# Loading a broadcast reciprocal over 128 partitions at once, and two weight loads moved in a queue

## The chip, the cores and the metric

The kernel runs on one core of a Trainium2 chip. The core has a matrix engine (TensorE, PE in the profile), a vector engine (VectorE, DVE), an activation engine (ScalarE, ACT), a general engine (GpSimd, POOL) and an engine that here only issues transfers (SyncE, SP). The engines run their own instruction streams in order and wait for one another by semaphores. Transfers between device memory and the on-chip memory of 128 partitions run on 16 DMA engines. The metric is the time of one execution on the device in microseconds (us), less is better.

## The reference

The program is one transformer block: layer norm with scale and shift from a conditioning vector, linear attention, then a second layer norm and a gated feed-forward network. Only the attention and the two gates matter here:

```python
mod = (_silu(c) @ w_mod).reshape(c.shape[0], 6, 1, -1)
sa, ca, ga, sb, cb, gb = (mod[:, i] for i in range(6))
h = _layernorm(x) * (1 + ca) + sa
# linear attention, 32 heads of 32
pq, pk = phi(q), phi(k)
kv = einsum('bhsd,bhse->bhde', pk, v);  z = einsum('bhsd->bhd', pk)
num = einsum('bhqd,bhde->bhqe', pq, kv)
den = einsum('bhqd,bhd->bhq', pq, z)[..., None] + 1e-06
x = x + ga * ((num / den) @ wo)
h = _layernorm(x) * (1 + cb) + sb
x = x + gb * ((_gelu(h @ w_gate) * (h @ w_up)) @ w_down)
```

There are 2,048 tokens of 1,024 features; the network's hidden width is 3,584. Inputs and outputs are bfloat16. In this listing the six slices and the transposes of the original are shortened.

## The kernel before, in words

Tokens are handled as 16 chunks of 128. Four chunks make a group (sg 0 to 3), and a group has two halves (h 0 and 1) of 256 tokens, `HW` in the code. The 1,024 features of q, k and the output are cut into 8 blocks g of 128, each with 4 heads (k 0 to 3, `HPG`) of 32.

The stages of the stretch in question come in this order. From about 128 us on, `m_tile` (matmuls at line 873) multiplies phi(k) transposed with the normed rows, in three column tiles for each g; 24 tiles run in all, first those of g 0 to 3, then the first tiles of g 4 to 7, then the others. ScalarE copies each result to `mb`; when the last tile of a g is copied, `m_t` has SP transpose it by DMA (line 678) into `mtb`, of which there are two buffers. `kv_prod` (matmuls at 891) multiplies that with the value weights, and VectorE masks it into `kvt` (895). `w2_pair` (1174) multiplies kvt with wo, which VectorE has first scaled by the first gate (`wofold`, 1180, from `gab`, a row that SP has loaded over all partitions at line 833). The list `HOOK` says after which tile each of these steps stands.

`den` (1201) computes the denominators of two groups on PE, 32 rows by 256 columns for each half of a group; VectorE adds 1e-6 and takes the reciprocal (1207), and SP stores the result to a scratch tensor in device memory, `scr_rd` (1209). `rb_load` (1221) then loads it back, so that each of the 32 partitions of a head holds that head's row: that is the broadcast over partitions. Its target `RB` is float32, has two buffers, one for even and one for odd groups, and holds two halves of 8 x 256 values for each partition. `pq_scale` (1234) multiplies phi(q) by it on VectorE, two g at a time, four instructions for a half. `wo_mm` (1242) multiplies the scaled phi(q) of a chunk with W2, in the order of g, and VectorE adds the result to x (1251, 1255). Chunks 0 and 1 belong to the first half of group 0, chunks 14 and 15 to the second half of group 3.

After this a chunk's second layer norm runs on ScalarE and GpSimd, and SP transposes it by DMA into `h2a` or `h2b` (678). VectorE and ScalarE scale and shift these, VectorE forms sums for the feed-forward products (`ss`, 1366, and `tp`, 1386, from the weights `wt` that SP loads at 1325), and PE starts the feed-forward (1411). In the first unit of the feed-forward, the list `ORD0` puts chunks 14 and 15 between the products, so their `wo_mm` (254.8 and 260.8 us) come last. The weights of the last matrix (`wd`, 1496) follow much later.

The second gate's row is made in two halves of 512 columns (j 0 and 1). For each, `gb_load` (761) loads two tiles `wmg` of 512 KiB from w_mod, and VectorE adds up eight weighted rows (`gb_acc`, 772 and 774). PE and SP turn the sums into a row that is stored to `scr_row` (827) and loaded over all partitions much later (`gbb`, 833). The first pair of loads is issued in tiles 1 and 2; the second load of each tile is issued as soon as its first content is used up.

All transfers of this stretch are issued by SP, in one queue and in the order of the program. SP has eight semaphores that its transfers use in turn; a transfer waits for the one eight places before it. The wait for a buffer stands in the same queue, so what is behind it waits too. The order of VectorE, ScalarE and GpSimd in this stretch isn't the program's: `reorder` simulates the stretch with a table of costs (`COST`) and due times and sorts the three engines' instructions by it. PE and SP keep the program's order.

Of the kernel before, what the change touches and what calls it, by code (L numbers as in the profile page):

```python
# [14 lines left out]
NSG = 4  # L15
CPG = NCH // NSG
SGW = P * CPG
NDC = D // P
NG = 8
HPG = 4  # L20
# [293 lines left out]
def bass_adaLN_cond__linear_attn_block__geglu_ffn__prompt_kernel(  # L314
# [12 lines left out]
    bf16, f32, f32r, i32 = dt.bfloat16, dt.float32, dt.float32r, dt.int32  # L327
    scr_row = nc.dram_tensor("scr_row", [3, 4, 512], f32).ap()
    scr_mod = nc.dram_tensor("scr_mod", [2, NDC, P], f32).ap()
    scr_rd = nc.dram_tensor("scr_rd", [NSG, 2, HPG, NG, SGW // 2 + 16], f32).ap()[:, :, :, :, 0:SGW // 2]  # L330
    with ExitStack() as es:
        es.enter_context(nc.allow_non_contiguous_dma(reason="1024 modulation values, laid out by partition"))
        arena = es.enter_context(nc.sbuf_tensor("arena", [P, ARENA_BYTES], dt.uint8, align_bytes=64))
# [4 lines left out]
        def at(name, shape, dty, off):  # L338
            return nc.alloc_sbuf_tensor_at(name, shape, dty, offset=ABASE + off, align_bytes=4)
# [33 lines left out]
        RB = [at(f"rb{i}", [P, 2, NG, SGW // 2], f32, OFF_RB[i]) for i in range(2)]  # L373
# [47 lines left out]
        def r_sm(name):  # L421
            return [(SMO[name], SMO[name] + SMSZ[name], name)]
# [30 lines left out]
        def r_wv(g):  # L453
            return [(OFF_WK + g * 2048, OFF_WK + (g + 1) * 2048, "wv")]
# [4 lines left out]
        def r_pq(sg, k0=0, k1=NG, s0=0, s1=SGW):  # L459
            return r_t8(PQO[sg], f"pq{sg}", k0, k1, s0, s1)  # L460
# [40 lines left out]
        def r_rb(i, h, g0=0, g1=NG):  # L501
            return [(OFF_RB[i] + (h * NG + g0) * 1024, OFF_RB[i] + (h * NG + g1) * 1024, f"rb{i}")]
# [17 lines left out]
        def pr(b):  # L520
            return [(b * 2048, (b + 1) * 2048)]
# [7 lines left out]
        sch = Sched()  # L529
        T, A, V, G, Q = PE_, ACT_, DVE_, POOL_, SP_  # L530
# [40 lines left out]
        def wm_dma(t, sl):  # L571
            return sch.dma(Q, lambda e: e.dma_start(WMST[sl][:], wm_v[:, :, t * 512:(t + 1) * 512]), wr=r_wm(sl), note=f"wm{t}")
# [22 lines left out]
        for q in range(1, 4):  # L595
            wmq_dma(q)
            for d0, d1 in ((2 * q, 2 * q + 1), (2 * q + 1, 2 * q + 2)):
# [8 lines left out]
               rd=r_sm("c8") + r_sm("ident"), pwr=pr(4))  # L606
# [4 lines left out]
               rd=r_sm("thc") + r_sm("chalf"), wr=r_sm("siluT"))  # L611
# [145 lines left out]
        def r_wmg(i, d0=0, d1=4):  # L757
            return [(HBO[3] + i * 4096 + d0 * 1024, HBO[3] + i * 4096 + d1 * 1024, f"wmg{i}")]

        def gb_load(j, q):  # L760
            sch.dma(Q, lambda e: e.dma_start(WMG[q][:], wm_v[:, 4 * q:4 * q + 4, (10 + j) * 512:(11 + j) * 512]), wr=r_wmg(q), note=f"wmg{j}.{q}")
# [6 lines left out]
        def gb_acc(j, dc):  # L768
            acc, rng = GA_[j]
            src, rs_ = WMG[dc // 4][:, dc % 4, :], r_wmg(dc // 4, dc % 4, dc % 4 + 1) + r_sm("silf")  # L770
            if dc == 0:
                sch.op(V, lambda e: e.tensor_scalar(acc[:, :], src, SILF[:, 0:1], None, op0=ALU.mult), rd=rs_, wr=rng, note=f"macc{6 + j}.0")
            else:
                sch.op(V, lambda e: e.scalar_tensor_tensor(acc[:, :], src, SILF[:, dc:dc + 1], acc[:, :], op0=ALU.mult, op1=ALU.add),
                       rd=rs_ + rng, wr=rng, note=f"macc{6 + j}.{dc}")
            if dc % 4 == 3 and j == 0:
                gb_load(1, dc // 4)

        def gb_hilo(j):
            acc, rng = GA_[j]  # L780
# [88 lines left out]
        def m_tile(g, k, bank, j):  # L869
            o_, n = MK[k]  # L870
            o = None
            for c_ in range(NCH):
                o = sch.op(T, lambda e, c_=c_: e.matmul(PS(bank, 0, n), PK[c_][:, g * P:(g + 1) * P], xrow(c_, o_, o_ + n),  # L873
                                                        start=(c_ == 0), stop=(c_ == NCH - 1)),
                           rd=r_pk(c_, g * P, (g + 1) * P) + r_xr(c_, o_, o_ + n), pwr=(pr(bank) if c_ == 0 else ()), note=f"m g{g} k{k} c{c_}")
            pset_writer(bank, o)
            w = n - (k == 0)
            sch.op(A, lambda e: e.activation(MB[g][:, o_:o_ + w], PS(bank, 0, w), ACTF.Copy), prd=pr(bank),
                   wr=[(OFF_MB[g] + o_ * 2, OFF_MB[g] + (o_ + w) * 2, f"mb{g}")], note=f"mcp{g}.{k}")
            if k == 0:  # L880
                sch.op(A, lambda e: e.activation(ZCOLS[:, g:g + 1], PS(bank, w, n), ACTF.Copy), prd=pr(bank), wr=r_smc("zcols", g, 4), note=f"zc{g}")

        def m_t(g):
            i = g % 2
            tdma(Q, MTB[i][:, :, :], MB[g][:, :], r_mb(g), r_mtb(i), f"mT{g}")
# [160 lines left out]
        def wofold(*kcs):  # L1046
            for kc in kcs:
                rg = r_wo(kc)
                sch.op(V, lambda e, kc=kc: e.tensor_tensor(WO[:, kc, :], WO[:, kc, :], GAB[:, :], ALU.mult),
                       rd=rg + R_GAB, wr=rg, note=f"wofold {kc}")  # L1050
# [66 lines left out]
        for c_ in range(10, NCH):  # L1117
            b = seq.index(("k", c_ // 2 * 2, 0)) - (9 if c_ % 2 else 12)
# [6 lines left out]
        for c_ in range(8, NCH, 2):  # L1125
            b = seq.index(("k", c_, 0)) - 3
# [10 lines left out]
        for g in range(NG):  # L1137
            task(nk + g // 2, lambda g=g: sch.dma(Q, lambda e: e.dma_start(WV[:, g, :, :], wqkv_v[:, :, 2 * D + g * P:2 * D + (g + 1) * P]),
                                                  wr=r_wv(g), note=f"wv{g}"))
# [54 lines left out]
        HW = SGW // 2  # L1194
# [16 lines left out]
            return store  # L1211

        o_rd = {}
        rb_ops = {}

        def rb_load(sg, hs=(0, 1)):
            i = sg % 2
            for h in hs:
                made = []
                for k in range(HPG):  # L1220
                    made.append(sch.dma(Q, lambda e, h=h, k=k: e.dma_start(  # L1221
                        RB[i][32 * k:32 * (k + 1), h, :, :],
                        scr_rd[sg, h, k:k + 1, :, :].to_broadcast([32, NG, HW])),
                        wr=r_rb(i, h) if k == 0 else (), deps=made[0].deps if k else [o_rd[sg // 2]], note=f"rb{sg}.{h}.{k}"))
                rb_ops[sg, h] = made

        GH = [((0, 2), (2, 4)), ((4, 6), (6, 8))]

        def pq_scale(sg, h, gs):
            i, t0 = sg % 2, h * HW  # L1230
            for g0, g1 in gs:
                ap = PQ[sg][:, g0:g1, t0:t0 + HW]
                rng = r_pq(sg, g0, g1, t0, t0 + HW)
                sch.op(V, lambda e, ap=ap, i=i, h=h, g0=g0, g1=g1: e.tensor_tensor(ap, ap, RB[i][:, h, g0:g1, :], ALU.mult),  # L1234
                       rd=rng + r_rb(i, h, g0, g1), wr=rng, deps=rb_ops[sg, h], note=f"pqs{sg}.{h}.{g0}")

        def wo_mm(c_, b0, gs):
            sg, ci = divmod(c_, CPG)
# [47 lines left out]
        for n, (g, k) in enumerate(tiles):  # L1286
            m_tile(g, k, n % 4, n % 2)
            if k == 2:
                m_t(g)
            for _ in range(3):  # L1290
                mod_step()
            if 2 <= n <= 9:
                wofold(n - 2)
            while pend and n > 1:
                wm_dma(*pend.pop(0))
            if n in (1, 2):
                gb_load(0, n - 1)
            for f in HOOK.get(n, "").split():
                hook_run(f)
        for i in range(4):  # L1300
            pq_scale(0, i // 2, GH[i % 2])
# [6 lines left out]
        kv_prod(7, 5)  # L1308
        w2_pair(6)
        rb_load(1)  # L1310
        x_dma(NXR, 10)
        wo_mm(2, 4, E6[:4])
# [356 lines left out]
```

## Time and profile before

| | |
|---|---|
| time, median of 3 runs | 806.04 us (804.77 to 806.11) |
| the profiled execution | 806.37 us, its span 804.5 us |
| granted TensorE clock | 1.00 in the whole span |
| bytes moved by DMA | 97.73 MB, mean 121 GB/s |
| rb loads | 32 of 256 KB, median 5.4 us from issue to landing |
| wmg loads | 4 of 512 KB, median 6.0 us |
| transposes into mtb | 8, median 5.1 us, longest 10.3 us |

The span is the time from the first to the last instruction of the program; the time on the clock is 1.87 us longer in the profiled execution. The profile gives each engine's busy time. PE's share is near the whole, so the rest of the profile is read for the short stretches in which PE isn't busy, and for what ended them.

The stretch around the change is seen best in the queue of SP. The columns are start, duration, engine and line, operation, target and source, and number of instructions; some rows are left out.

```profile
136.42 0.35 SPq L833 DMA_DIRECT2D gab<-scr_row  x1
136.83 0.42 SPq L761 DMA_DIRECT2D wmg<-in_w_mod_dram  x1
137.35 1.28 SPq L678 DMA_TRANSPOSE mtb<-mb  x1
138.73 0.52 SPq L572 DMA_DIRECT2D wmst<-in_w_mod_dram  x1
139.30 3.31 SPq L761 DMA_DIRECT2D wmg<-in_w_mod_dram  x1
142.71 0.45 SPq L572 DMA_DIRECT2D wmst<-in_w_mod_dram  x1
143.26 9.25 SPq L678 DMA_TRANSPOSE mtb<-mb  x2
163.44 0.37 SPq L761 DMA_DIRECT2D wmg<-in_w_mod_dram  x1
163.92 1.24 SPq L678 DMA_TRANSPOSE mtb<-mb  x1
...
178.75 2.01 SPq L1221 DMA_DIRECT2D rb<-scr_rd  x4
181.91 1.23 SPq L678 DMA_TRANSPOSE mtb<-mb  x1
183.19 2.08 SPq L1221 DMA_DIRECT2D rb<-scr_rd  x4
...
196.06 3.93 SPq L1221 DMA_DIRECT2D rb<-scr_rd  x8
...
213.13 2.01 SPq L1221 DMA_DIRECT2D rb<-scr_rd  x4
```

Here the wmg loads stand between the gab load and the second transpose, and the third wmg load ahead of the transpose of g 3. Each half of the broadcast is four issues. Three further groups of four rb loads, at 223.1, 226.6 and 241.0 us, stand between the transposes of h2 and the loads of x and wt.

### The profile page before, as it was taken

Reading aid. Unit: us, or ns where it says so; the run is one execution under the profiler, and the core shown is the slowest. Engines: PE = TensorE matmul, PEld = TensorE weight load, DVE = VectorE, ACT = ScalarE, POOL = GpSimd, SP = SyncE. Lnnn points to the kernel's source line nnn. Section 1 sums busy time; section 2 is a strip of 40 time slices with the busy share of each in tenths; the row PEclk is TensorE's granted clock in tenths of the full one; section 3 lists DMA queues with packets and bytes.
Section 4 is the critical chain, followed back from the end, with each engine's and each line's share of the span. In section 5 each row is a group of like instructions: output and inputs, shape, how many; then the busy total and the mean of one; then the engine's idle time right before and its main releaser. Section 6 shows DMA issues by size and latency. Waiting matters only on the chain.

```text
span 804.5 us, 10875 instructions
## 1 busy us (share of the span) xinstructions
PE 792.9 (99%) x4029; PEld 465.3 (58%) x4029; DVE 568.1 (71%) x1008; ACT 303.1 (38%) x511; POOL 39.4 (5%) x102
## 2 busy tenths in 40 slices
PE   7999999999999999999999999999999999999998
PEld 4444445666444677767775444467776777744445
DVE  6699898984699978788786375577887878601422
ACT  2497743232655444344443410033544435300000
POOL 2121200000320000000000000000000000000000
PEclk9999999999999999999999999999999999999999
DMA  9789859749898135323237324022231323430100
GB/s 282 242 176 231 176 116 230 186 98 184 186 265 225 53 112 150 98 61 104 58 101 235 53 74 110 20 86 76 82 105 53 106 72 86 136 126 7 53 20 27
DMA packets 168508, 97.73 MB, mean 121 GB/s; under 512 B 68476, under 2 KB 156804, under 8 KB 168456
## 3 DMA queue, kind: packets, MB, share of 16 engines
q1 hardware_dynamic: 168440, 97.04, 47.0%
q8 instruction: 32, 0.52, 0.3%
q14 instruction: 20, 0.16, 0.1%
q10 hardware_dynamic: 16, 0.00, 0.0%
HBM read 78.92 MB, written 4.47 MB: 104 GB/s over the span
## 4 chain that ended last, share of the span: by engine, by line
PE 84%; DMA 6%; SPq 4%; DVE 3%; issue 1%; ACT 1%; POOL 0%; DVEq 0%; POOLq 0%; ACTq 0%
PE ps_all L1411 43%; PE ps_all L1496 24%; PE ps_all L909 7%; PE ps_all L858 6%; PE ps_all L873 3%; DMA rb<-scr_rd 3%; DMA mtb<-mb 1%; SPq L575 1%; DVE pq L1234 1%; DMA wmq<-in_w_mod_dram 1%; SPq L580 1%; DVE ss L1366 1%; SPq L1221 1%; DMA scr_row<-mrowa 1%; SPq L678 1%
## 5 line engine op out<-in xcount | busy, mean ns | idle before, releaser
L1411 PE MATMUL ps_all<-ss,tp 128*128 128x512 f32 x896 | 224.7, 402 | 1.2 <-DVE ss L1366 1.2
L1496 PE MATMUL ps_all<-wd,yT 128*128 128x512 bf16 (+3 forms) x952 | 193.9, 366 | 0.0
L1411 PEld LDWEIGHTS ps_all<-ss,tp 128*128 128x128 f32 x896 | 168.2, 188 | 42.4 <-DVE ss L1366 2.6
L1496 PEld LDWEIGHTS ps_all<-wd,yT 128*128 128x128 bf16 x952 | 90.0, 98 | 103.8 <-ACT ge L1427 0.5
L1427 ACT ACTIVATE ge<-ps_all 128x512 f32<-128x512 f32 x112 | 64.2, 597 | 144.7 <-DVE ps_all L1422 79.7
L1411 PE MATMUL ps_all<-h2a,wt 128*128 128x512 bf16 x448 | 106.2, 380 | 0.4 <-DVE xall L1255 0.4
L1386 DVE TENSOR_TENSOR tp<-wt 128x512 fp32r<-128x512 bf16 x112 | 74.3, 688 | 39.6 <-PE ps_all L1411 20.8
L1431 DVE TENSOR_TENSOR yT<-ge,ps_all 128x512 bf16<-128x512 f32 x112 | 74.7, 685 | 34.4 <-PE ps_all L1411 31.0
L1422 DVE TENSOR_TENSOR ps_all<-ps_all,es 128x512 f32<-128x512 f32 x112 | 75.3, 696 | 16.1 <-PE ps_all L1411 16.1
L1488 DVE TENSOR_TENSOR ps_all<-ps_all,gbb 128x512 f32<-128x512 f32 (+3 forms) x34 | 22.7, 668 | 79.0 <-PE ps_all L1496 79.0
L1386 DVE TENSOR_TENSOR tp<-wt,tp 128x512 fp32r<-128x512 bf16 x112 | 72.0, 684 | 0.0
L1411 PEld LDWEIGHTS ps_all<-h2a,wt 128*128 128x128 bf16 x448 | 39.4, 98 | 55.0 <-issue 14.8
L1242 PE MATMUL ps_all<-w,pq 128*128 128x512 bf16 x256 | 56.5, 379 | 1.6 <-DVE pq L1234 1.6
L858 PE MATMUL ps_all<-wk,h1T 128*128 128x512 bf16 x248 | 56.8, 379 | 0.3 <-DVE h1T L699 0.2
L909 PE MATMUL ps_all<-h1T,wq 128*128 128x512 bf16 x256 | 56.7, 379 | 0.0
L1411 PE MATMUL ps_all<-ar,tp 128*128 128x512 f32 x224 | 55.3, 389 | 0.0
L1416 ACT ACTIVATE ps_all<-ps_all 128x512 f32<-128x512 f32 x56 | 32.6, 582 | 53.2 <-PE ps_all L1411 51.4
L847 ACT ACTIVATE eb<-ps_all 128x512 f32<-128x512 f32 x64 | 36.4, 594 | 37.7 <-PE ps_all L858 15.6
L1411 PEld LDWEIGHTS ps_all<-ar,tp 128*128 128x128 f32 x224 | 42.0, 188 | 8.7
L1242 PEld LDWEIGHTS ps_all<-w,pq 128*128 128x128 bf16 x256 | 24.7, 98 | 32.0 <-DVE pq L1234 2.3
L909 PEld LDWEIGHTS ps_all<-h1T,wq 128*128 128x128 bf16 x256 | 24.9, 98 | 30.0
L1419 ACT ACTIVATE es<-ps_all 128x512 f32<-128x512 f32 x56 | 33.5, 601 | 18.6 <-PE ps_all L1411 18.6
(118 smaller groups left out, 638.0 us busy)
## 6 DMA issues: line engine op xcount, KB each, us to landing
wt<-in_B_w_gate_dram SPq DMA_DIRECT2D x28, 512.0 KB, 4.2
wt<-in_B_w_up_dram SPq DMA_DIRECT2D x28, 512.0 KB, 4.9
wd<-in_B_w_down_dram SPq DMA_DIRECT2D x12, 1024.0 KB, 7.3
rb<-scr_rd SPq DMA_DIRECT2D x32, 256.0 KB, 5.4
wmst<-in_w_mod_dram SPq DMA_DIRECT2D x6, 1024.0 KB, 5.6
wmq<-in_w_mod_dram SPq DMA_DIRECT2D x8, 512.0 KB, 6.1
out_dram<-xall SPq DMA_DIRECT2D x31, 128.0 KB, 1.7
xall<-in_A_x_dram SPq DMA_DIRECT2D x5, 512.0 KB, 4.1
```

The lines of the kernel that those rows point to most:

```text
L847: sch.op(A, lambda e: e.activation(EB[i][:, :], PS(bank), ACTF.Exp), prd=pr(bank), wr=rng, note=f"{note}.exp")
L858: o = sch.op(T, lambda e, dc=dc: e.matmul(PS(bank), H1[sg][:, ci, dc, :], W_[:, dc, jg * 512:(jg + 1) * 512], start=(dc == 0), stop=(dc == ...
L909: o = sch.op(T, lambda e, dc=dc: e.matmul(PS(b), WQ[:, dc, qc * P:(qc + 1) * P], H1[sg][:, :, dc, :], start=(dc == 0), stop=(dc == NDC - 1 ...
L1242: last[half] = sch.op(T, lambda e, g=g, half=half: e.matmul(PS(b0 + half), PQ[sg][:, g, ci * P:(ci + 1) * P], W2[:, g, half * 512:(half + ...
L1386: sch.op(V, lambda e, t=t: e.tensor_tensor(TP[k][:, t, :, :], in0[:, t, :, :], in1[:, t, :, :], ALU.subtract), rd=r0[t:t + 1] + (r1[t:t + ...
L1411: o = sch.op(T, lambda e, l_=l_, r_=r_, dc=dc: e.matmul(PS(b), l_, r_, start=fresh and dc == 0, stop=dc == ND2 - 1, skip_group_check=True) ...
L1416: sch.op(A, lambda e: e.activation(PS(BB + t), PS(BA + t), ACTF.Copy), prd=pr(BA + t), pwr=pr(BB + t), note="pcp")
L1419: sch.op(A, lambda e: e.activation(ES[t][:, :], PS(BE + t), ACTF.Copy), prd=pr(BE + t), wr=r_2k(OFF_ES[t], f"es{t}"), note="escp")
L1422: sch.op(V, lambda e: e.tensor_tensor(PS(dst + t), PS(BB + t), ES[t][:, :], ALU.add), prd=pr(BB + t), rd=r_2k(OFF_ES[t], f"es{t}"), pwr=pr ...
L1427: sch.op(A, lambda e: e.activation(GE[i][:, :], PS(b), ACTF.Gelu_apprx_tanh), prd=pr(b), wr=r_2k(OFF_GE[i], f"ge{i}"), note="gelu")
L1431: sch.op(V, lambda e: e.tensor_tensor(YT[:, yrow(fc), h * SGW:(h + 1) * SGW], GE[i][:, :], PS(b + 1), ALU.mult), rd=r_2k(OFF_GE[i], f"ge{i ...
L1496: o = sch.op(T, lambda e, fc=fc: e.matmul(PS(b, 0, n), YT[:, yrow(fc), ci * P:(ci + 1) * P], WDT[fc // 4][:, fc % 4, c0:c1], start=first a ...
```

## The change

The change has three parts. First, `rb_load` loads a half with two transfers in place of four. Each covers all 128 partitions and four of the eight blocks g, and its source pattern has three levels: the four heads k, 32 repeats of each, and 1,024 values in one piece. `pq_scale` now waits only for the transfer that holds its own blocks. Second, the scratch tensor loses the 16 values of padding that followed each row of 256. Third, the wmg loads move in SP's queue: the first pair is issued in tiles 6 and 7, behind the transpose of g 1, and the second pair in tile 11, behind that of g 3.

```diff
-    scr_rd = nc.dram_tensor("scr_rd", [NSG, 2, HPG, NG, SGW // 2 + 16], f32).ap()[:, :, :, :, 0:SGW // 2]
+    scr_rd = nc.dram_tensor("scr_rd", [NSG, 2, HPG, NG, SGW // 2], f32).ap()
...
-            if dc % 4 == 3 and j == 0:
-                gb_load(1, dc // 4)
...
         def rb_load(sg, hs=(0, 1)):
             i = sg % 2
             for h in hs:
-                made = []
-                for k in range(HPG):
-                    made.append(sch.dma(Q, lambda e, h=h, k=k: e.dma_start(
-                        RB[i][32 * k:32 * (k + 1), h, :, :],
-                        scr_rd[sg, h, k:k + 1, :, :].to_broadcast([32, NG, HW])),
-                        wr=r_rb(i, h) if k == 0 else (), deps=made[0].deps if k else [o_rd[sg // 2]], note=f"rb{sg}.{h}.{k}"))
-                rb_ops[sg, h] = made
+                for q in range(2):
+                    src = scr_rd[sg, h, :, 4 * q:4 * q + 4, :].rearrange("k (o g) t -> k o (g t)", o=1).to_broadcast([HPG, 32, 4 * HW])
+                    sch.dma(Q, lambda e, h=h, q=q, src=src: e.dma_start(RB[i][:, h, 4 * q:4 * q + 4, :].rearrange("p a b -> p (a b)"), src),
+                            wr=r_rb(i, h, 4 * q, 4 * q + 4), deps=[o_rd[sg // 2]], note=f"rb{sg}.{h}.{q}")
...
-                       rd=rng + r_rb(i, h, g0, g1), wr=rng, deps=rb_ops[sg, h], note=f"pqs{sg}.{h}.{g0}")
+                       rd=rng + r_rb(i, h, g0, g1), wr=rng, note=f"pqs{sg}.{h}.{g0}")
...
-            if n in (1, 2):
-                gb_load(0, n - 1)
+            if n in (6, 7):
+                gb_load(0, n - 6)
+            if n == 11:
+                gb_load(1, 0)
+                gb_load(1, 1)
```

Since the planner simulates the new transfers, it also puts some of VectorE's instructions in another order: the product of the mask with z, two of the folds of wo, the reciprocal of the second pair of groups and the masks of kvt 5 to 7 stand elsewhere. The masks of kvt 5 to 7 now follow all eight `pq_scale` instructions of group 0. On ScalarE the copies into `mb` and the roundings of the sums change places a few times. The order of PE is the same.

More of the change, by code (lines that the diff above doesn't have):

```diff
@@ L1213, in bass_adaLN_cond__linear_attn_block__geglu_ffn__prompt_kernel @@
         o_rd = {}
-        rb_ops = {}
         def rb_load(sg, hs=(0, 1)):
```

## The prediction

> **What bounds the kernel now.** I read the busy times first, then the chain of waits, then the timelines of TensorE (PE), VectorE (DVE) and the SyncE queue (SP) between 125 and 262 us, where the change lies, and last the DMA view over short windows.
>
> ```profile
> span 804.5 us, 10875 instructions
> PE 792.9 (99%) x4029; PEld 465.3 (58%) x4029; DVE 568.1 (71%) x1008; ACT 303.1 (38%) x511; POOL 39.4 (5%) x102
> ```
>
> PE is busy 99% of the span, so an edit can win only PE's gaps, but it can lose as much as it holds PE up. The PE timeline names the gaps in this stage; the bracket at the end of a row gives the idle time before it and who ended it.
>
> ```profile
> 153.58 0.62 PE L891 MATMUL ps_all<-mtb,wv 128*128 128x128 bf16 x8 [1.11 <-DMA mtb<-mb]
> 231.87 13.99 PE L1242 MATMUL ps_all<-w,pq 128*128 128x512 bf16 x64 [1.59 <-DVE pq L1234]
> 254.84 3.63 PE L1242 MATMUL ps_all<-w,pq 128*128 128x512 bf16 x16
> ```
>
> Further gaps of 0.44, 0.72, 0.17 and 0.30 us lie at 246.3, 250.6, 252.9 and 258.8: 4.33 us in all. That is the most the change can win. The rb loads are ahead of two DVE stalls and of the 1.59 us gap:
>
> ```profile
> 220.73 2.50 DVE L1234 TENSOR_TENSOR pq<-pq,rb 128x512 bf16<-128x512 bf16 x4 [3.00 <-DMA rb<-scr_rd]
> 231.12 2.50 DVE L1234 TENSOR_TENSOR pq<-pq,rb 128x512 bf16<-128x512 bf16 x4 [1.14 <-DMA rb<-scr_rd]
> 252.76 2.49 DVE L1234 TENSOR_TENSOR pq<-pq,rb 128x512 bf16<-128x512 bf16 x4
> ```
>
> The DMA engines are the second limit: from 213 to 258 us their busy share is 111.9%. So what a load costs the queue matters. Four windows price it: 131 to 136.4 us (the end of the two wo loads, and the four-row store of mrowa), 137 to 141.2 (the gab load, then wmg), 198.4 to 206 (rb loads alone), 248.4 to 250.7 (the gbb load between wt loads).
>
> ```profile
> DMA packets 806, 1.57 MB, mean 291 GB/s; under 512 B 36, under 2 KB 40, under 8 KB 806
> DMA packets 510, 0.89 MB, mean 212 GB/s; under 512 B 25, under 2 KB 382, under 8 KB 510
> DMA packets 1755, 1.69 MB, mean 222 GB/s; under 512 B 105, under 2 KB 1755, under 8 KB 1755
> DMA packets 656, 0.88 MB, mean 381 GB/s; under 512 B 32, under 2 KB 474, under 8 KB 655
> ```
>
> Present price: 1 MiB of rb (one half of one group of four chunks) at 222 GB/s is 4.7 us; eight such halves are 8 MiB. The first row holds something more. Its 36 smallest packets are no data; two loads over 128 rows and one store over 4 rows ended there, and 36 = 16 + 16 + 4. I read them as one completion word per DMA engine that took part: 16 engines for a transfer whose outermost count is 128, 4 for one whose outermost count is 4.
>
> **The change, part by part.**
>
> *The rb loads.* Each half becomes 2 DMAs of 512 KiB instead of 4 of 256 KiB. That takes two SP issues of about 0.45 us from each half (a group of four takes 2.01 us), lets the first two scalings of a half start when half its bytes are there, and makes the packets 4 KiB instead of 1 KiB. But the source pattern changes too. Before, its outermost count was 32 (one row of 1/den repeated 32 times). Now it is 4 (k), then 32 repeats, then 1,024 floats; the destination still counts 128. If the smaller outermost count decides, as in the four-row store, only 4 of the 16 engines carry 1/den.
>
> Price on 4 engines: gbb is the row most like the new load (512 KiB, 4 KiB packets, one row repeated over partitions). Its window ran at 381 GB/s, 23.8 per engine; times 4 that is 95.3 GB/s, so 1 MiB takes 11.0 us. The bad end is the gab window, the same kind of load at 212 / 16 = 13.25 per engine: 19.8 us. On 16 engines 1 MiB takes 2.75 us (381) to 4.9 (212). I take 4 engines at 11.0 us.
>
> [...]
>
> Now the queue. Every later DMA puts a sixteenth of itself on each of the four slow engines, behind the rb packets there, so those four set the pace. From the first rb half (issued 178.75; gab's bytes began to move about 1.2 us after issue, so 180.0) to the end of the last, they carry 8 x 11.0 = 88.0 us of rb. Queued between are 11 transposes of 256 KiB (three mtb, eight h2), x loads of 1,792 KiB, wt loads of 1,024 KiB and the 128 KiB store: 5.9 MB at 264 GB/s, the mean of 131 to 147 us, 22.3 us. End: 180.0 + 88.0 + 22.3 = 290.3. For this the four must never run dry. The closest call is h2a's first transpose, which needs chunk 0. DVE now puts kvt5 to kvt7 behind all eight scalings of group 0, so W2 of g 5 (PE at 193.3) waits until the second half lands at 180 + 22.0 + 1.4 = 203.4, near 204.5: 11 us late. The transpose (issued 211.8) then comes at about 223, while the four engines have work until about 228. It holds.
>
> What is late next: the scalings of chunks 14 and 15 need the last half. PE reaches that point at 254.84 now and finishes chunk 14 at 258.47. Then: last bytes at 290.3, one scaling 0.63, the remaining four g of chunk 14 at 8 x 0.216 (a chunk's 16 matmuls take 3.45 us) = 1.73, end 292.7: 34.2 us late. DVE's sums of h2 stand ahead of these scalings and themselves wait for h2 transposes queued behind rb; they take 0 to 2 us more, I take 0.8. After that nothing is left to hide the loss, because PE has no gap from 264 us on. Sum: 804.5 + 35.0 = 839.5 us of span. The span stands 1.5 us below the median shown (806.04), so the forecast is 841 us.
>
> *w_mod loads of the second gate.* Two wmg loads (1 MiB) leave the queue ahead of the transpose mtb of g 1, which takes 10.28 us from issue to landing and causes the 1.11 us gap. At 264 GB/s they are worth 4.0 us of its wait, so the gap goes: -1.11 us on PE. Their own landing is hidden: the first use is at 158.9 on DVE, and from 155 to 165 us the DMA share is 0.04, so all that is queued here ends before. Without this cover DVE, which has no idle from 141.4 to 172, would wait up to the 4.0 us. The second pair now issues after the transpose of g 3, whose issue no longer waits at 163.44 for DVE's sums; kv3 on PE was not waiting for it, so it wins nothing. This gain starts the rb queue at most 1.1 us earlier; I leave it inside the range.
>
> *Planner and padding.* DVE moves the z product and two folds of wo, and puts the second reciprocal behind two scalings; its store leaves SP at 195.4, 10 us after the reciprocal, so that is hidden in front of rb1. Dropping 64 bytes of padding leaves the stores' bytes the same: 0.
>
> **The rivals.**
>
> *A, all 16 engines carry the new loads (it ends faster).* For it: the destination counts 128. Against: the four-row store. A half then takes 2.75 us, the waits for rb vanish, and up to 4.33 us of gaps go: 800.2 to 804 of span, 801.7 to 805 on the clock. It decides as long as 1 MiB stays under the 4.7 us of today. 11%.
>
> *B, four engines for each load, but different ones in turn.* Consecutive halves then overlap and 1 MiB costs about 2.75 to 5.5 us: 804.5 to 807.5. Nothing in the profile speaks for it; the four-row stores show the number of engines, not which. 4%.
>
> *C, four engines at the lower rate of gab.* 8 x (19.8 - 11.0) = 70 us on top: 911. For it: rb itself runs at 13.9 per engine. Against: four engines read four different rows here, and gbb, with all on one row, ran at full rate. 5%.
>
> *D, 16 engines, but kvt5 behind the scalings costs PE 1 to 3 us:* 806 to 809. 2%. The forecast itself has 78%.
>
> **How the numbers follow.** The likeliest case alone lies between 825 and 866: rb rows overlap by 12.9% in busy share (-10 us), the other loads may pass at some 346 GB/s, as in the last slices of 131 to 147 us (-5); up to 14.2 us per MiB, midway in rate between gab and gbb, adds 25. The range goes to 880 for part of C and leaves out A, B and D and the tails, about 2 in 10: 825 to 880. About 0.2% (1.6 us) is what a measurement of this kernel can tell from no change. Faster: A, 11%. Same: most of B, 4%. Slower: the forecast, C, D and the rest, 85%.
>
> **What would show it.** Right: rb landings of 10 us and more; DMA busy share near 0.3 while rb moves, at about 95 GB/s; PE gaps before L1242 that sum to some 35 us between 190 and 295, ended by the scalings or by transposes; no gap at 153.6 before L891. Wrong: rb windows near 381 GB/s and a DVE without waits at the scalings (then A), or a share near 0.3 with PE not held up (then the queue does not run in order).

## The result, and the profile after

| | before | after |
|---|---|---|
| time, median of the runs beside each other | 806.08 us (804.77 to 806.18, 4 runs) | 852.95 us (852.07 to 854.16, 4 runs) |
| ratio, 95% interval | | 1.0591 (1.0578 to 1.0604) |
| span of the profiled execution | 804.5 us | 850.3 us |
| granted TensorE clock, mean | 1.00 | 0.974 |

The kernel became 5.9% slower; the span grew by 45.8 us. The busy times on the page of the kernel after:

```profile
PE 804.7 (95%) x3962; PEld 469.4 (55%) x4029; DVE 569.0 (67%) x1008; ACT 302.9 (36%) x511; POOL 38.1 (4%) x102
```

PE's share fell from 99% to 95%, and its busy time rose although the work is the same. Both mean lost time: the first is idle time, the second is slower matmuls. VectorE's timeline shows what it waited for. Columns: start, duration, engine and line, operation, tiles, count, and in brackets the idle time before and who ended it.

```profile
242.27 1.29 DVE L1228 TENSOR_TENSOR pq<-pq,rb 128x512 bf16<-128x512 bf16 x2 [6.03 <-DMA rb<-scr_rd]
247.27 1.29 DVE L1228 TENSOR_TENSOR pq<-pq,rb 128x512 bf16<-128x512 bf16 x2 [3.70 <-DMA rb<-scr_rd]
...
298.16 1.29 DVE L1228 TENSOR_TENSOR pq<-pq,rb 128x512 bf16<-128x512 bf16 x2 [3.71 <-DMA rb<-scr_rd]
```

The two loads of a half land 5.00 us apart, so 512 KiB take 5.0 us and a half of 1 MiB takes 10.0 us, against 4.7 us before. Fourteen such waits add up to 49.6 us. The last two scalings, for which chunks 14 and 15 wait, start at 298.16 us. The DMA view of the stretch from 196 to 205 us, in which most of one half of 1/den moves beside little else, gives the rate:

```profile
DMA packets 856, 0.94 MB, mean 105 GB/s; under 512 B 665, under 2 KB 669, under 8 KB 855
q1 hardware_dynamic: 855, 0.93, 30.8%
```

The 16 engines are busy for 30.8% of that stretch, though a load is under way for nearly all of it. Rate and share are those of 4 or 5 engines out of 16. The completion words that the prediction counted decide between the two. The end of one load in the kernel after (198.4 to 199.2 us) and of one in the kernel before (199.3 to 199.9 us):

```profile
DMA packets 24, 0.08 MB, mean 102 GB/s; under 512 B 4, under 2 KB 4, under 8 KB 24
DMA packets 131, 0.12 MB, mean 196 GB/s; under 512 B 16, under 2 KB 131, under 8 KB 131
```

The packets under 512 B, of 4 bytes each, are the completion words: 4 now, 16 before. PE's timeline shows what this did to the matmuls:

```profile
206.58 0.63 PE L1172 MATMUL ps_all<-wo,kvt 128*128 128x512 bf16 x1 [9.17 <-DVE kvt L893]
...
259.50 3.60 PE L1236 MATMUL ps_all<-w,pq 128*128 128x512 bf16 x8 [4.34 <-DVE pq L1228]
277.26 5.35 PE L1236 MATMUL ps_all<-w,pq 128*128 128x512 bf16 x24 [3.11 <-DVE pq L1228]
298.91 3.08 PE L1236 MATMUL ps_all<-w,pq 128*128 128x512 bf16 x8 [3.11 <-DVE pq L1228]
```

Twelve gaps between 192 and 304 us, four of them shown, sum to 34.3 us, against 4.33 us of gaps before: 30.0 us more. The rows also show slower matmuls: 8 of them take 3.60 or 3.08 us, where a chunk's 16 took 3.45 us before. The view by windows shows why; its columns are the stretch, the busy time of each engine with its count, the granted clock, the DMA share and the rate:

```profile
195.00:205.00 10.00, 2.42 (x10) 1.06 (x8) 1.67 (x3) 0.46 (x1) 0.00 (x0) 0.67 0.31 102
215.00:225.00 10.00, 9.95 (x48) 4.42 (x47) 5.85 (x11) 3.94 (x5) 1.70 (x5) 1.00 0.52 146
300.00:306.00 6.00, 5.02 (x12) 2.91 (x11) 6.00 (x8) 0.60 (x1) 0.00 (x0) 0.50 0.80 226
```

Where PE waited, the mean granted clock of the window fell to 0.67; where it was fed (215 to 225 us), it was 1.00. It stayed at 0.50 for a while after the last wait. The busy time of PE is best compared with a kernel in whose trace as many matmul records, 67 of 4,029, are missing: the last experiment below has 3,962 as well, and 788.2 us. The slow clock thus made PE's work some 16.5 us longer. Gaps and slower work together are 30.0 + 16.5 = 46.5 us, within 0.7 us of the growth of the span.

### The profile page after: what moved, and what is told of

It is laid out like the page before. It is cut to its first block, busy times and chain, and to the rows that moved or that the text cites. A ratio compares the mean times of both kernels' runs of the same rounds, so it can differ in the third digit from the quotient of the medians.

```text
span 850.3 us, 10784 instructions
## 1 busy us (share of the span) xinstructions
PE 804.7 (95%) x3962; PEld 469.4 (55%) x4029; DVE 569.0 (67%) x1008; ACT 302.9 (36%) x511; POOL 38.1 (4%) x102
## 3 DMA queue, kind: packets, MB, share of 16 engines
q1 hardware_dynamic: 161848, 97.03, 49.6%
## 4 chain that ended last, share of the span: by engine, by line
PE 82%; SPq 7%; DMA 7%; DVE 1%; issue 1%; ACT 1%; POOL 0%; ACTq 0%; POOLq 0%; DVEq 0%
PE ps_all L1408 41%; PE ps_all L1493 23%; PE ps_all L907 7%; PE ps_all L871 6%; SPq L678 5%; PE ps_all L856 4%; DMA rb<-scr_rd 4%; DMA h2a<-xl 2%; PE ps_all L1236 2%; SPq L575 1%; DMA wmq<-in_w_mod_dram 1%; SPq L580 1%; SPq L1218 0%; ACT xl L649 0%; SPq L569 0%
## 5 line engine op out<-in xcount | busy, mean ns | idle before, releaser
L1408 PE MATMUL ps_all<-h2a,wt 128*128 128x512 bf16 x420 | 101.6, 384 | 4.2 <-DVE xall L1249 2.2
L1236 PE MATMUL ps_all<-w,pq 128*128 128x512 bf16 x251 | 67.1, 427 | 18.8 <-DVE pq L1228 18.4
L1236 PEld LDWEIGHTS ps_all<-w,pq 128*128 128x128 bf16 x256 | 26.5, 107 | 58.5 <-DVE pq L1228 23.6
L1228 DVE TENSOR_TENSOR pq<-pq,rb 128x512 bf16<-128x512 bf16 x32 | 20.6, 688 | 49.6 <-DMA rb<-scr_rd 49.6
```

What stands on the lines that cost most here:

```text
L1236: last[half] = sch.op(T, lambda e, g=g, half=half: e.matmul(PS(b0 + half), PQ[sg][:, g, ci * P:(ci + 1) * P], W2[:, g, half * 512:(half + ...
L1408: o = sch.op(T, lambda e, l_=l_, r_=r_, dc=dc: e.matmul(PS(b), l_, r_, start=fresh and dc == 0, stop=dc == ND2 - 1, skip_group_check=True) ...
```

## The experiments

All times stand beside runs of the kernel before on the same chip (medians of 805.2 to 805.6 us).

**1. Only the w_mod loads moved.**

```diff
 (before)
-            if dc % 4 == 3 and j == 0:
-                gb_load(1, dc // 4)
...
-            if n in (1, 2):
-                gb_load(0, n - 1)
+            if n in (6, 7):
+                gb_load(0, n - 6)
+            if n == 11:
+                gb_load(1, 0)
+                gb_load(1, 1)
```

> The rb loads, the padding and the waits of the kernel before; only the w_mod loads of the second gate are moved behind the transposes. Theory (the rb loads alone cost the 47 us): 1.1 us faster than before at most, 804.5 to 806.5 us, no gap of PE before L891 at 153.6. Rival (the moved w_mod loads, or the order of VectorE that the planner makes of them, carry part of the loss): more than 3 us slower than before.

Measured: 804.72 us (804.00 to 805.88, 11 runs), ratio 0.9994 (0.9985 to 1.0003). No difference that can be told: the moves carry none of the loss, and no gain that shows.

**2. Only the loads of 1/den changed** (the kernel after, with `gb_load` where it was before).

```diff
 (after)
-            if n in (6, 7):
-                gb_load(0, n - 6)
-            if n == 11:
-                gb_load(1, 0)
-                gb_load(1, 1)
+            if n in (1, 2):
+                gb_load(0, n - 1)
...
+            if dc % 4 == 3 and j == 0:
+                gb_load(1, dc // 4)
```

> The new rb loads and no padding, with the w_mod loads where they were before. Theory: the whole loss, 851 to 856 us, each 512 KiB of rb in 5.0 us. Rival (as for the run with the w_mod loads alone): clearly under 850 us.

Measured: 853.46 us (851.64 to 854.53, 4 runs), ratio 1.0596 (1.0581 to 1.0611). The new loads carry the whole loss.

**3. Four copies of 1/den, so that the source's outermost count is 16.** The loads keep their number, their 128 partitions and their 4 KiB packets; SP issues four stores where it issued one.

```diff
 (after)
-    scr_rd = nc.dram_tensor("scr_rd", [NSG, 2, HPG, NG, SGW // 2], f32).ap()
+    scr_rd = nc.dram_tensor("scr_rd", [NSG, 2, HPG, 4, NG, SGW // 2], f32).ap()
...
-    src = scr_rd[sg, h, :, 4 * q:4 * q + 4, :].rearrange("k (o g) t -> k o (g t)", o=1).to_broadcast([HPG, 32, 4 * HW])
+    src = scr_rd[sg, h, :, :, 4 * q:4 * q + 4, :].rearrange("k r (o g) t -> (k r) o (g t)", o=1).to_broadcast([16, 8, 4 * HW])
```

> As the changed kernel, but 1/den is stored four times (four stores for one), so that the loads' source pattern is 16 rows, 8 repeats, 1,024 values: 128 partitions and 4 KiB packets as before, outermost count 16 instead of 4. Theory (the outermost count of the source sets the number of DMA engines, 4 in the changed kernel): 16 engines, 1 MiB in 2.7 to 4.9 us, VectorE's waits for rb nearly gone, PE's clock full, 800 to 806 us. Rival 1 (4 KiB packets of a repeated row, or the lost padding, are slow whatever the count): 845 us or more. Rival 2 (the destination's count of 128 differs from the source's, and that alone makes the transfer slow): 845 us or more too.

Measured: 809.11 us (806.99 to 809.56, 5 runs), ratio 1.0038 (1.0024 to 1.0052), above the theory's 800 to 806. VectorE's timeline and the DMA view of 187.5 to 192 us of this kernel:

```profile
190.77 1.29 DVE L1228 TENSOR_TENSOR pq<-pq,rb 128x512 bf16<-128x512 bf16 x2 [1.43 <-DMA rb<-scr_rd]
193.06 1.29 DVE L1228 TENSOR_TENSOR pq<-pq,rb 128x512 bf16<-128x512 bf16 x2 [0.99 <-DMA rb<-scr_rd]
```

```profile
DMA packets 313, 1.05 MB, mean 234 GB/s; under 512 B 57, under 2 KB 57, under 8 KB 313
q1 hardware_dynamic: 313, 1.05, 104.6%
```

A load now lands 2.29 us after the one before it, not 5.00, it ends in 16 completion words (189.59 to 189.70 us), all engines are busy, and almost the whole loss is gone. So it was the source's outermost count of 4 that made the loads slow, not their 128 partitions nor their size. But the rate is only about that of the old loads over 32 partitions (222 GB/s), and the kernel is still 0.4% slower than before.

**4. Two copies, outermost count 8.**

```diff
 (after, as in 3 with 2 in place of 4)
+    src = scr_rd[...].rearrange("k r (o g) t -> (k r) o (g t)", o=1).to_broadcast([8, 16, 4 * HW])
```

> The same with two copies: 8 rows, 16 repeats, 1,024 values. Theory: 8 engines, so 512 KiB in about 2.5 us and 1 MiB in 5.0 us, close to the 4.7 us of the kernel before: 803 to 812 us. Rivals 1 and 2: 845 us or more. If the number of engines isn't set by the count, no value between the run with four copies and the changed kernel is explained.

Measured: 834.61 us (833.81 to 835.29, 4 runs), ratio 1.0364 (1.0350 to 1.0378), far above what was expected. VectorE's timeline and the DMA view of 191.5 to 199.5 us of this kernel:

```profile
195.42 1.29 DVE L1228 TENSOR_TENSOR pq<-pq,rb 128x512 bf16<-128x512 bf16 x2 [4.32 <-DMA rb<-scr_rd]
199.82 1.29 DVE L1228 TENSOR_TENSOR pq<-pq,rb 128x512 bf16<-128x512 bf16 x2 [3.11 <-DMA rb<-scr_rd]
```

```profile
DMA packets 494, 0.89 MB, mean 111 GB/s; under 512 B 294, under 2 KB 294, under 8 KB 494
q1 hardware_dynamic: 494, 0.89, 52.7%
```

The share of 52.7% is that of 8 engines, as expected, and a load ends in 8 completion words (194.18 to 194.24 us). But 512 KiB take 4.40 us, hardly less than on 4 engines: twice the engines, each at little more than half the rate. The trace's packet records say the same: over the first 14 loads, a 4 KiB packet of 1/den has a median of 159 ns in the kernel after, 285 ns here and 273 ns with four copies. Per 1 MiB that is 64 packets an engine x 159 ns = 10.2 us, 32 x 285 = 9.1 and 16 x 273 = 4.4.

**5. The kernel before without its padding.**

```diff
 (before)
-    scr_rd = nc.dram_tensor("scr_rd", [NSG, 2, HPG, NG, SGW // 2 + 16], f32).ap()[:, :, :, :, 0:SGW // 2]
+    scr_rd = nc.dram_tensor("scr_rd", [NSG, 2, HPG, NG, SGW // 2], f32).ap()
```

> The kernel before with the 16 values of padding taken out of scr_rd and nothing else, so that a row of 1/den is 8 KB in one piece instead of 8 pieces of 1 KB. Theory (the padding is no part of the loss; the loads of 32 partitions still go to all engines): 803 to 808 us, 256 KB in 1.2 us as before (about 220 GB/s), no wait for rb above 3.1 us. Rival (the padding is what kept these loads on all engines, and the change lost by taking it out): a load falls to 4 engines or fewer and the time is over 830 us.

Measured: 805.39 us (804.33 to 806.88, 10 runs), ratio 1.0000 (0.9991 to 1.0009). The padding is no part of it.

**6. One load of 1/den issued earlier, in the kernel after.** SP's rows in the kernel after had suggested a second loss. A transpose queued behind a slow load holds SP for 4 to 12 us, so that the next load is issued late:

```profile
226.79 4.35 SPq L678 DMA_TRANSPOSE h2a<-xl  x1
231.24 1.16 SPq L1218 DMA_DIRECT2D rb<-scr_rd  x2
232.49 10.60 SPq L678 DMA_TRANSPOSE h2a<-xl  x1
...
249.93 1.16 SPq L1218 DMA_DIRECT2D rb<-scr_rd  x2
251.18 8.38 SPq L678 DMA_TRANSPOSE h2a<-xl  x1
```

```diff
 (after)
         x_dma(NXR, 10)
+        rb_load(2, (0,))
...
-        SLOT = {2: lambda: (pq_scale(1, 0, GH[0] + GH[1]), rb_load(2, (0,))),
+        SLOT = {2: lambda: (pq_scale(1, 0, GH[0] + GH[1]),),
```

> The kernel after, with the load of half 0 of group 2 issued right behind the load of x that follows group 1's loads, ahead of the first transpose of h2 (in the kernel after it is issued at 231.24 us, behind that transpose). Theory (besides the slow loads themselves, the change loses time because SP is held inside a transpose for 4 to 12 us until the slow engines have drained, so that the next load is issued to idle engines): the load of half 2.0 no longer starts 4 to 5 us after the one before it has landed, its last part lands near 242.5 instead of 247.3 us, the later ones follow 3 to 6 us earlier, and the time is 847 to 850 us. Rival (only the bytes over the slow engines count, wherever they are issued): the last part lands at 298 us again, 852 to 854 us.

Measured: 850.63 us (849.87 to 854.42, 4 runs), ratio 1.0571 (1.0549 to 1.0593); the kernel after has 1.0591 (1.0578 to 1.0604), so the two can't be told apart; the time lies between the ranges of the two theories. VectorE's timeline of this kernel:

```profile
238.86 1.29 DVE L1228 TENSOR_TENSOR pq<-pq,rb 128x512 bf16<-128x512 bf16 x2 [3.28 <-DMA rb<-scr_rd]
243.86 1.29 DVE L1228 TENSOR_TENSOR pq<-pq,rb 128x512 bf16<-128x512 bf16 x2 [3.71 <-DMA rb<-scr_rd]
257.22 1.29 DVE L1228 TENSOR_TENSOR pq<-pq,rb 128x512 bf16<-128x512 bf16 x2 [5.32 <-DMA rb<-scr_rd]
```

The half that was moved lands 3.4 us earlier (243.86 against 247.27). But the time from its landing to the next half's first, less the 5.0 us of a load alone, grows from 6.48 to 8.36 us (257.22 - 5.00 - 243.86), and the last load gains only 1.1 us (297.09 against 298.16). The transposes that it was moved past only moved into the next stretch.

**7. Packets of 2 KiB, four loads a half, in the kernel after.**

```diff
 (after)
-    for q in range(2):
-        src = scr_rd[sg, h, :, 4 * q:4 * q + 4, :]...to_broadcast([HPG, 32, 4 * HW])
+    for q in range(4):
+        src = scr_rd[sg, h, :, 2 * q:2 * q + 2, :]...to_broadcast([HPG, 32, 2 * HW])
```

> The kernel after with four loads a half instead of two, each of 2 of the 8 groups: packets of 2 KB instead of 4 KB, the outermost count of the source still 4. Theory (the number of engines that share a load follows the outermost count of its source, so 4 engines carry it whatever the packets are): a half of 1 MiB takes 10 to 11.5 us again, in four steps of 2.5 to 2.9 us, 850 to 856 us, with up to 3 us for the longer issue. Rival (the rate is a matter of packets, or of how many loads are in flight): a half of 1 MiB takes under 8 us or over 13, and the time is under 845 or over 865 us.

Measured: 848.14 us (846.24 to 848.72, 4 runs), ratio 1.0527 (1.0512 to 1.0541). The four loads of a half land 2.57 us apart (189.15, then 191.72 us on VectorE's timeline), 10.3 us a half: the rate stays with the outermost count. The time lies between the two ranges, below the theory's 850 and above the rival's 845. The last load lands at 292.74 us instead of 298.16. From one load ahead of the first landing (2.6 us before 183.85 here, 5.0 us before 186.87 in the kernel after) to there, eight halves at the rate of a load alone take 8 x 10.3 = 82.4 us, which leaves 29.1 us for all else; the same sum for the kernel after, with 8 x 10.0, leaves 36.3. Why less is left with smaller loads was not tried.

**8. The kernel before with both loads of group 2 issued earlier.**

```diff
 (before)
         x_dma(NXR, 10)
+        rb_load(2)
...
-        SLOT = {2: lambda: (pq_scale(1, 0, GH[0] + GH[1]), rb_load(2, (0,))),
+        SLOT = {2: lambda: (pq_scale(1, 0, GH[0] + GH[1]),),
...
-                4: lambda: (cb1(), rb_load(2, (1,))),
+                4: lambda: (cb1(),),
```

> The kernel before, with both loads of group 2 issued right behind the load of x that follows group 1's loads (SP then waits some 11 us for the layer norm, and the DMA engines rest at 205 to 211 us), instead of between the transposes of h2. Theory (in the stretch of 178 to 258 us the time is set by when 1/den lands): DVE's waits of 3.0 us for rb at about 230 us go, chunk 14 ends 1 to 4 us earlier than 258.5 us, 801 to 804.5 us. Rival (the stretch is set by the layer norm's and the transposes' own chain, and the loads only fill its waits): the waits move to h2a and the time stays within 804 to 807 us; if the transposes of h2 are held behind the 2 MiB, 806 to 809 us.

Measured: 802.54 us (801.48 to 803.69, 7 runs), ratio 0.9968 (0.9957 to 0.9979): faster than both kernels. VectorE's timeline of this kernel, with the rows that answer to the waits of 3.00 and 1.14 us before, and its list of PE's waits from 150 to 330 us:

```profile
215.85 2.49 DVE L1234 TENSOR_TENSOR pq<-pq,rb 128x512 bf16<-128x512 bf16 x4
226.57 2.49 DVE L1234 TENSOR_TENSOR pq<-pq,rb 128x512 bf16<-128x512 bf16 x4
```

```profile
PE ps_all L1412 <- DVE ss L1367: 0.8, 3, 0.4
```

Both waits are gone, and of the 4.33 us of gaps 0.8 are left. The gap of 1.11 us at 153.6 us is missing here too, though SP's order ahead of it is the same; that part isn't the edit's gain. Before, these 2 MiB were issued among the transposes and the wt loads; now they move while SP would only wait for the layer norm.

**9. The loads of 1/den on ScalarE's queue, in the kernel after.**

```diff
 (after)
-    LANES = {SP_: 8, POOL_: 4, ACT_: 2}
+    LANES = {SP_: 8, POOL_: 4, ACT_: 8}
...
-                    sch.dma(Q, lambda e, h=h, q=q, src=src: e.dma_start(
+                    sch.dma(A, lambda e, h=h, q=q, src=src: e.dma_start(
```

> The kernel after, with its 16 loads of 1/den issued by ScalarE's DMA queue (8 of them may be under way) in place of SP's; the transposes and the other loads stay on SP's. The 4 engines and the bytes are the same. Theory (a good part of the loss is that loads and transposes share one queue: SP is held inside a transpose for 4 to 12 us, the next load is issued late, and the transposes land behind 1 MiB of slow load): the stretches between two loads of 1/den shrink, the last part lands at 280 to 290 us instead of 298, and the time is 832 to 845 us. Rival (the 4 engines themselves set the pace, and the other transfers' share of them fills the stretches between, on whichever queue): the last part lands at 294 us or later and the time is 848 us or more; if ScalarE's own work is held behind the loads, more.

Measured: 875.56 us (873.06 to 878.52, 4 runs), ratio 1.0874 (1.0836 to 1.0913): slower still, and the last part lands at 322.11 us. SP's rows and then PE's rows of this kernel:

```profile
175.91 19.15 SPq L678 DMA_TRANSPOSE mtb<-mb  x3
...
271.24 16.80 SPq L678 DMA_TRANSPOSE h2a<-xl  x2
```

```profile
202.06 1.01 PE L889 MATMUL ps_all<-mtb,wv 128*128 128x128 bf16 x8 [13.46 <-DMA mtb<-mb]
...
290.89 15.96 PE L1236 MATMUL ps_all<-w,pq 128*128 128x512 bf16 x64 [27.36 <-DVE pq L1228]
```

No load of 1/den stands in SP's queue any more, and SP is held in its transposes all the same. The theory of the shared queue falls, and the rival's reading, that the transposes wait for the 4 engines and not for SP's queue, fits. Two loads now land 6.8 us apart (196.00 - 189.17 on VectorE's timeline) instead of 5.0, while SP's transposes move beside them. ScalarE also stood still for 23.2 us ahead of its last `mb` copy, behind the loads of group 1, so not all of the extra time is the DMA engines', and a queue whose engine has no other work wasn't tried.

**10. One row to 128 partitions, written as 16 times 8.** Only gab's and gbb's loads in the kernel before are changed.

```diff
 (before)
-    scr_row[row, a0:a0 + 2, :].rearrange("(o a) b -> o a b", o=1).to_broadcast([P, 2, 512])
+    scr_row[row, a0:a0 + 2, :].rearrange("(o x a) b -> o x (a b)", o=1, x=1).to_broadcast([16, 8, 1024])
```

> The kernel before, with its two loads of one 4 KB row to all 128 partitions (gab and gbb) written as 16 times 8 instead of 128: the shape of the loads with four copies of 1/den. This measures one thing, the duration of a 4 KB packet. Theory (a load whose source's outermost count is 16 gives each engine 8 partitions in a row, and packets are slower in that pattern than where the outermost count is 128): packets of 250 to 280 ns as with four copies, against 166 ns in the kernel before, and gbb's 512 KiB take 2.5 to 3.2 us instead of 2.0. Rival (the slower packets come from the many different rows or from what runs beside them): 160 to 175 ns and 2.0 us. The time of the kernel stays within 804 to 808 us in either case, since neither load is waited for more than 1 us longer.

Measured: 805.26 us (one run). The trace's packet records of gbb, 128 packets of 4 KiB in each:

```
                      first start to last end      sum       median packet
before (128)          248.59 to 250.60 us          21.2 us   166 ns
this kernel (16 x 8)  247.26 to 251.34 us          32.8 us   282 ns
```

The same row, the same destination, and a shape that in experiment 3 ended in 16 completion words: a packet of gbb takes 1.7 times as long. So slow packets come with the shape; how it is shared out over the engines is not shown. The shape isn't all of it: gab's packets were slow in the kernel before too, with nothing beside them up to 139.4 us (median 252 ns written as 128, 308 ns as 16 times 8; 3.4 and 3.6 us for the load). gbb's load of 512 KiB took 4.1 us, longer than the 2.5 to 3.2 expected; other transfers ran beside it, and it was seen once.

**11. Four copies, with group 2 issued earlier** (experiment 3 with the edit of experiment 8).

```diff
 (experiment 3)
         x_dma(NXR, 10)
+        rb_load(2)
```

> The kernel with four copies of 1/den (16 loads over 16 engines, w_mod loads moved; 809.1 us), with both loads of group 2 issued ahead of the transposes of h2, the edit that took the kernel before from 805.3 to 802.5 us. Theory (what the four copies still lose is small waits for 1/den and transposes between 180 and 240 us; once group 2 is early, DVE's waits at 219 and 230 us go and the 16 loads are as good as the 32): 802 to 805 us. Rival (four stores and two halves in place of one keep their price whatever comes after: 3 to 4 us above the kernel before with the same edit): 805.5 to 808 us.

Measured: 804.85 us (803.18 to 807.91, 12 runs), ratio 1.0002 (0.9990 to 1.0014). The earlier issue wins back the 0.4%, and the time lies in the theory's range; but 2.3 us remain to experiment 8, so 16 such loads are not as good as the 32. PE's waits in this kernel are:

```profile
PE ps_all L1172 <- DVE kvt L893: 2.3, 1, 2.3
PE ps_all L889 <- DMA mtb<-mb: 1.4, 1, 1.4
```

Together 3.7 us, at 181 and 196 us; experiment 8 has neither. They stand ahead of all scalings but those of group 0: the last transposes of the KV products, and kvt behind the scalings on VectorE. No run tried to take them away.

**12. The w_mod moves with group 2 issued earlier** (experiment 1 with the edit of experiment 8).

```diff
 (experiment 1)
         x_dma(NXR, 10)
+        rb_load(2)
```

> The kernel before with the loads of group 2 issued early (802.5 us in its run) and, besides, the change's moves of the w_mod loads. Theory (those moves carry nothing either way): 801.5 to 803.5 us, no difference from the early loads alone. Rival (they take away TensorE's wait of 1.11 us at 153.6 us, which counts once nothing behind it waits): 800.5 to 801.7 us.

Measured: 801.97 us (801.75 to 804.08, 5 runs), ratio 0.9966 (0.9954 to 0.9977), beside 0.9968 (0.9957 to 0.9979) without the moves: no difference that can be told. The early loads are the gain.

## Where the prediction was right, and where a size was off

*The mechanism was right.* The forecast was 841 us, from 825 to 880; it came to 852.95. That the source's outermost count of 4 decides, not the destination's 128, is shown by experiments 2 and 3: the loads alone give 1.0596, and with a count of 16 almost all of it is gone. The completion words follow the count: 4, 8 and 16 for a load with 4, 8 and 16 outermost. Another transfer did leave a part of itself behind 1/den on the four: of the 384 packets of the x load that SP issued at 208.91 us, 288 moved from 217.93 to 221.64 us and ended in 12 completion words. The other 96, four sixteenths, moved from 230.37 to 234.02 us, starting as the four words of the last 1/den load there came (230.37, 230.61, 231.12 and 232.08 us). The sign, the chain (late 1/den, late scalings, gaps on PE ahead of L1236) and the end at chunk 14 came as written.

*The price of a load alone was 1.0 us too high.* 1 MiB took 10.0 us instead of 11.0. But on its way, with other transfers beside it, a half took 12.3 us on average, and here the sum was too small.

*The step that failed is the sum "8 x 11.0 = 88.0 us of rb" plus 22.3 us for what is queued between, laid end to end, with "For this the four must never run dry".* The trace's packet records of the kernel after show when 1/den moved (its 4 KiB packets, and the completion words of the last half):

```
1/den moves           us      halves   then none for
179.52 to 191.27      11.75   1         0.87 us
192.14 to 204.03      11.89   1         3.73
207.76 to 232.09      24.33   2         2.73
234.82 to 246.69      11.87   1         5.34
252.03 to 263.16      11.13   1         0.87
264.03 to 275.90      11.87   1         6.43
282.33 to 297.65      15.32   1
sum                   98.16   8        19.97
```

The start came 0.5 us earlier than the 180.0 forecast. The halves took 10.2 us more than 88.0, and the stretches with no 1/den 2.3 us less than 22.3. VectorE saw the last landing 0.5 us after the last packet, at 298.16 us: 7.9 us behind the 290.3. The mis-sized term is thus the loads themselves, beside other transfers. The first load of a half, with transposes or x beside it, took 5.9 to 6.7 us instead of 5.0; in the last half, with the loads of x, gbb and wt beside it, 9.9 us (282.33 to 292.24). That these transfers slow the loads is read from the records; no run tried it apart.

In the stretches without 1/den the others moved 4.5 MB. At 264 GB/s that is 17.1 us, so slow or empty engines cost about 2.9 us of the 20.0. The DMA views of two of them, from 246.7 to 252.0 us and from 232.1 to 234.8:

```profile
DMA packets 3651, 1.44 MB, mean 272 GB/s; under 512 B 1603, under 2 KB 3651, under 8 KB 3651
...
DMA packets 656, 0.24 MB, mean 88 GB/s; under 512 B 615, under 2 KB 615, under 8 KB 656
```

The first ran at the rate assumed; in the second little moved. I took these stretches for a fault of SP's order, and SP did issue late: the second store of 1/den, priced at nothing in the prediction, left at 205.32 us, 15.5 us after its reciprocal had ended, since SP was held in transposes. But experiments 6 and 9 don't bear out that the order is the loss: an earlier issue moved the time to the next stretch, and another queue made it worse.

*The end.* With the last half at 298.16 instead of 290.3 (+7.9), a tail of 3.83 us to the end of chunk 14 (298.91 + 3.08 - 298.16) instead of 0.63 + 1.73 (+1.5), no separate 0.8 for VectorE's sums, and 2.3 us more from chunk 14 to the end (548.3 against 546.0), 35.0 becomes 45.9; measured, 45.8.

*Missing from the prediction: the clock.* It reckoned each matmul at the old 0.216 us. After each wait some groups took up to twice that. Of the 16.5 us found above, most fills time in which PE would else have waited for the next half of 1/den, since the landings set the pace; on the path I count the 1.5 us of the tail and most of the last 2.3. That division is reckoned from the rows; no run tried it. The clock records of the kernel after have 0.50 from 299.47 to 306.30 us, after a wait of 3.11 us that ended at 298.91 (more in the last section).

*kvt behind the scalings* was priced well: W2 of g 5 ran at 206.58 us (204.5 forecast), and the first transpose of h2 was issued at 226.79 (223).

*The w_mod moves:* the gap at 153.6 us did go, worth 1.11 us by its row, but in experiment 1 the medians differ by 0.6 us, and the interval takes in no gain at all. The gap itself varies: in kernels that leave these loads in place it was 0.57 us (experiment 10), 0.45 (2), 0.16 (5) and nothing (8), so 1.11 us was the most to be had. It is absent in every kernel profiled with the moves. *Padding:* 0, as reckoned.

*Rival A's price was wrong.* It said 801.7 to 805 us with all 16 engines, at 381 GB/s; with 16 engines the loads ran at about the old 222 GB/s and the kernel of experiment 3 took 809.11. The step that led there, from gbb's rate over 128 partitions to any load over 128 partitions, doesn't hold: gbb's source has an outermost count of 128, and in experiment 10 gbb's packets took 1.7 times as long without it (gab's 1.2 times).

## What to carry to other kernels

Look at the outermost count of the source of a broadcast load, not only of its destination: turning four loads over 32 partitions into two over 128, with k outermost, cut the engines from 16 to 4, and the rate from 222 to 105 GB/s. Count what shares those engines too: transposes waited behind the loads (one held SP for 11.67 us) and, by the packet records, slowed them in turn (with transposes or x beside it, the first load of a half took 5.9 to 6.7 us instead of 5.0), and ScalarE's queue did not help (875.56 us). A sum of transfers laid end to end, each priced as if alone, was too small here: 110.3 us reckoned from the first to the last of 1/den, 118.1 measured. And where a queue is full, ask first whether it rests somewhere: moving 2 MiB of loads into the 11.2 us in which SP waits for the layer norm won 0.3% (802.54 us), and no new shape of the load tried here did.

## What the runs showed of the hardware

More engines did not mean more rate in proportion. With a source of 4, 8 and 16 outermost (128 partitions, 4 KiB packets), 512 KiB took 5.00, 4.40 and 2.29 us, and a packet 159, 285 and 273 ns; with 128 outermost and one row (gbb), 166 ns. In experiment 10 the same row written as 16 times 8 had packets of 282 ns; no run here shows which partitions an engine wrote, so the cause is open. Packets on 4 engines were slow as well when other loads ran beside them: in the last half 0.31 us each (9.9 us for 32 an engine). Why they weren't slow alone (159 ns) is open.

A transpose queued behind loads on 4 engines held the issuing engine for up to 11.67 us, where the transposes of h2 took 1.2 to 3.8 us each before, and they held it even with the loads on another engine's queue (19.15 us for three transposes, 16.80 for two in experiment 9).

The granted clock followed marks 3.41 us apart: the stretches at 0.50 in the clock records of the kernel after last 3.41, 6.83 or 10.24 us. Three windows between such marks, with PE's busy time as the first number behind the length and the clock third from the end:

```profile
275.58:278.99 3.41, 1.73 (x8) 0.80 (x9) 1.47 (x3) 0.00 (x0) 0.00 (x0) 1.00 0.97 271
...
282.41:285.82 3.41, 1.17 (x5) 0.51 (x6) 3.41 (x5) 3.31 (x7) 0.00 (x0) 1.00 0.47 116
285.82:289.23 3.41, 3.25 (x9) 1.18 (x9) 3.41 (x8) 2.24 (x4) 0.00 (x0) 0.50 1.10 216
```

After 1.73 us of work in a window the clock stayed at 1.00; after 1.17 us it fell to 0.50, and after 3.25 us it came back. So it went in the 37 windows from 186.83 to 313.12 us of the kernel after: full clock fell after the six in which PE had been busy for at most 1.17 us, and after none of the 18 with 1.73 us or more; from 0.50 it came back after the six with 3.25 us or more, and not after the seven with at most 2.52 us. A wait of 3.11 us that a mark cut in two (274.15 to 277.26 us) cost no clock, and one of 2.25 us inside a window (282.61 to 284.86) did.
